# Attention and MLP on one core: half-width left sums in one bank, one key transpose a unit, and a re-ordered tail

## The chip, the cores and the metric

The kernel runs on one core of one Trainium2 chip. The metric is device time in microseconds of one execution. TensorE (PE in the profile, PEld for its weight loads) multiplies; VectorE (DVE), ScalarE (ACT) and GpSimd (POOL) do the element-wise work; SyncE (SP) and POOL issue most DMA transfers. The program gives each engine its own list of instructions, in an order written out by hand, with semaphores between the engines.

## The reference

```
q, k, v: (8, 12, 448, 64) fp32        batch, heads, sequence, head width
q_n = q / sqrt(mean(q*q) + 1e-6) * g_q        (over the head width)
k_n = k / sqrt(mean(k*k) + 1e-6) * g_k
attn = softmax(q_n @ k_n^T / 8)               448 x 448 for each head
x = concat over heads of (attn @ v)           (8, 448, 768)
xn = (x - mean) / sqrt(var + 1e-6) * g_ln     (LayerNorm over 768)
out = x + relu(xn @ w1) @ w2                  w1 768 x 3072, w2 3072 x 768
```

## The kernel before

**Pairs and steps.** Two heads make a pair; six pairs make a batch; 48 pairs in all, in units of one or two pairs that are loaded and prepared together. The 448 keys of a head are three blocks of 128 and a left block of 64; the two left blocks of a pair are stacked into one of 128. So a pair has seven steps: three blocks of head 0, three of head 1, and the common left block. Scores come out transposed, keys on the partitions and 448 queries along the row (`score`, L461); ScalarE takes the exponential into a row buffer E (`power`, L503); then E is the stationary operand of the value sums.

**Value sums** (`value`, L524 to L544). For each step there are four matmuls, with 128 columns of E as weights and 65 columns of values streamed (64 and a column of ones, for the softmax denominator); the seventh step streams 130, both heads at once. The first three go to query blocks 0, 1 and 2 in bank `oA`. The fourth takes E columns 320:448, a full width of 128, into bank `oB`; of its result only the lower half (queries 384:448) is used. There is one `oA` and one `oB`. After the seventh step `evac_o` (L546) takes the reciprocals of the denominators (L555, L556) and multiplies (L557, L562), into the batch's token tiles `x` (three tiles of 128 tokens) and `xl` (64 left tokens; two batches share one such tile). The next pair's first sum waits for that. The first batch's six pairs go by another function (L791), with banks of its own.

**Preparation of a unit** (`pieces`). Squares on ScalarE into `khl` (a, c), their sums on DVE (d, e), roots (g), keys weighted on POOL (i, L324), split into a high and a low half on POOL and DVE (j, k), queries scaled (l) and doubled (m). Then SP issues DMA transposes of keys (x, `dma_k`, L351 and L354) and queries (y, `dma_q`, L361 and L364), from the ninth unit on. Keys take three transfers: twelve groups at once, and the left groups in two halves of 64 partitions. The next unit's squares overwrite `khl`, so they wait for those transposes. `PLAN` gives each piece a step, counted from two pairs before the unit's first pair, the same for all units; Q, K and V in it are the loads (Q and K of the next unit, V of this one).

**MLP.** While attention of batch b + 1 runs, the MLP of batch b does (`run_rest`): it emits one product chunk (six matmuls), then as many attention steps as its share says, so that they are done `tails` chunks before the end of the batch's chunks. In the last chunks there is only the second product and, in pieces of `LN_AT`, LayerNorm of the next batch (`ln_list`). A batch with odd b has four token tiles (its own three and the shared left one), one with even b three. The up-product is L1126 with Relu on ScalarE (L1128). The down-product (`products`) goes by a seven-product scheme in place of eight for each two token tiles: sums of hidden halves are formed first (`sums_of`), and seven products are added into the two tiles with signs and shared terms, at chunk offsets given by `AFTER`. Product 1 is kept by a ScalarE copy (`keep`, L1238), products 6 and 7 are added to it (`second`, L1247), and `spread` (L1254) adds the kept sum into the tiles, one half of a tile at a time. For the second pair of tiles the kept sum lies in two row buffers of E.

**Where the order comes from.** It is all written by hand: `ORDER` for the first 110 us, then `PLAN`, `AFTER`, `LN_AT`, `tails` and the shares in `run_rest`.

Of the kernel before, what the change touches and what calls it, by code (L numbers as in the profile page):

```python
# [71 lines left out]
PLAN = [(-8, "bai"), (-7, "d"), (-6, "c"), (-5, "ej"), (-4, "g"), (-3, "lk"), (0, "QmKx"), (1, "V"), (2, "y")]  # L72
AFTER = ((2, 1, 5, 5, 7, 9, 9, 10, 10, 13, 11, 12, 14), (1, 2, 3, 5, 7, 7, 9, 10, 10, 11, 12, 15, 14), (1, 2, 5, 9, 8, 8, 9, 10, 10, 15, 14, 12, 14), (10, 14), (6, 7))
LN_AT = ((0, 3, 3, 6, 7), (0, 1, 2, 4, 4, 4))
# [49 lines left out]
class _Fast:  # L124
# [158 lines left out]
    def pieces(self, u):  # L283
# [64 lines left out]
        def dma_k():  # L348

            khl, kU = c["khl"].rearrange("p g e d -> p g (e d)"), self.kU[u % 2]  # L350
            nc.sync.dma_start_transpose(  # L351
                kU[:, 0:1536].rearrange("p (g c) -> p g c", c=128), khl[:, 0:12])
            for e in range(2):
                nc.sync.dma_start_transpose(  # L354
                    kU[:, 1536:1920].rearrange("p (w c) -> p w c", w=2)[
                        :, :, 128 * e:128 * e + D], khl[64 * e:64 * e + 64, 12:14])

        def dma_q():
# [6 lines left out]
            for w in range(2):  # L365
                self.prs[p0 + w] = dict(
                    q=qU[:, w].rearrange("p e s -> p (e s)"),
                    main=self.kU[u % 2][:, 768 * w:768 * w + 768],
                    left=self.kU[u % 2][:, 1536 + 192 * w:1728 + 192 * w])
# [110 lines left out]
    def left_score(self, p):  # L480
# [8 lines left out]
        for e in range(2):  # L489
            nc.tensor.matmul(ps[64 * e:64 * e + 64, 0:S], left[:, 128 * e:128 * e + 64],  # L490
# [28 lines left out]
    def values(self, p, i):  # L519
        self.value(p, i)  # L520
        if i == 6:
            self.evac_o(p)

    def value(self, p, i):  # L524
# [6 lines left out]
        oA, oB = c["oA"], c["oB"]  # L531
        if i < 6:
            h, j = divmod(i, 3)
            rhs = self.v16[:, p % 6, h, j]
            cs = slice(65 * h, 65 * h + 65)
        else:
            rhs = self.vl[:, p % 6].rearrange("p e d -> p (e d)")
            cs = slice(0, 130)
        for t in range(3):
            nc.tensor.matmul(oA[:, t, cs], E[:, ts(t, 128)], rhs,  # L540
                             start=(i == 0 and t == 0), stop=(i == 6 and t == 2))
        nc.tensor.matmul(oB[:, cs], E[:, 320:448], rhs, start=(i == 0), stop=(i == 6))  # L542
# [3 lines left out]
    def evac_o(self, p):  # L546
# [5 lines left out]
        oA = c["oA"].rearrange("p t (e d) -> p t e d", e=2)  # L552
        oB = c["oB"].rearrange("p (e d) -> p e d", e=2)
        rec = self.rec[:, p]
        nc.vector.reciprocal(rec[:, 0:3], oA[:, :, :, D])  # L555
        nc.vector.reciprocal(rec[64:128, 3], oB[64:128, :, D])  # L556
        nc.vector.tensor_tensor(  # L557
            out=x[:, :, 128 * hp:128 * hp + 128].rearrange("p t (e d) -> p t e d", e=2),
            in0=oA[:, :, :, 0:D], in1=rec[:, 0:3].unsqueeze(3).broadcast_to([128, 3, 2, D]),
            op=ALU.mult)  # L560
        r0 = 64 * (b % 2)
        nc.vector.tensor_tensor(  # L562
            out=xl[r0:r0 + 64, 128 * hp:128 * hp + 128].rearrange("p (e d) -> p e d", e=2),
            in0=oB[64:128, :, 0:D], in1=rec[64:128, 3].unsqueeze(2).broadcast_to([64, 2, D]),
            op=ALU.mult)
# [407 lines left out]
    def attention(self):  # L973
# [3 lines left out]
        for u in range(4, nu):  # L977
# [3 lines left out]
            for at, names in PLAN:  # L981
# [12 lines left out]
        for p in range(nb0, n + 1):  # L994
            for i in range(7):
                c = []
                if i == 0 and p < n and p % NPAIR == 0 and p > nb0:
# [14 lines left out]
                if p > nb0 + 1 and i == 1 and (p - 1) % NPAIR and p > 2 * NPAIR:  # L1012
# [122 lines left out]
    def after_up(self, b, f):  # L1135
# [4 lines left out]
        if f in (8, 14):  # L1140
            self.sums_of(0, "3", slice(0, 6) if f == 8 else slice(6, 12), self.xn)
        if f == 20:
# [29 lines left out]
    def products(self, b, n):  # L1172
# [51 lines left out]
        homes, flat = {}, self.rows.rearrange("p k s -> p (k s)")  # L1224

        def kept(a):
# [4 lines left out]
            return six(flat[:, S * homes[a]:S * homes[a] + 768].bitcast(FP32))  # L1231

        def keep(key, a):
            def call():
                if a:
                    k = homes[a] = next(k for k in range(8) if {k, k + 1} <= set(self.free_rows))
                    self.free_rows = [y for y in self.free_rows if y not in (k, k + 1)]
                nc.scalar.activation(kept(a), six(c[key][:, 0:384]), AFT.Identity)  # L1238
            return call

        def leave(a):
            self.free_rows += [homes[a], homes[a] + 1]

        def second(key, a):
            def call():
                u = kept(a)
                tt(out=u, in0=six(c[key][:, 0:384]), in1=u, op=ALU.add)  # L1247
                self.free(c.pop(key))
            return call

        def spread(t, g, a):
            def call():
                u, x = kept(a), six(tiles[t][:, 384 * g:384 * g + 384])
                stt(out=x, in0=u, scalar=self.rs[:, b, t:t + 1], in1=x, op0=ALU.mult, op1=ALU.add)  # L1254
# [15 lines left out]
        def pair(a):  # L1270
# [10 lines left out]
            places = dict(zip(("S2", "r1", "r2", "S4", "r5", "s5", "u2", "x2", "u3", "y3", "z3", "r4", "r3"), at))  # L1281
            if a == 0:
                after(h, lambda: self.sums_of(0, "1", slice(6, 12)))
            after(h + 1, keep(key(1), a))
            todo_of = dict(
                S2=sums(a, "2"), r1=read(key(1), a, L), r2=read(key(2), a, L), S4=sums(a, "4"),
                r5=read(key(5), a, R, last=False), s5=read(key(5), a + 1, R), u2=second(key(6), a),
                x2=spread(a, 1, a), u3=second(key(7), a), y3=spread(a + 1, 0, a), z3=spread(a + 1, 1, a),
# [3 lines left out]
            if a:  # L1292
# [319 lines left out]
```

## Time and profile before

| | |
|---|---|
| three runs | 612.62, 608.44, 611.16 us (median 611.16) |
| profiled execution, its own time | 609.88 us |
| its span | 608.3 us |
| granted TensorE clock, mean | 0.99 |
| TensorE busy | 566.9 us, 93% |
| VectorE, ScalarE, GpSimd busy | 398.3, 345.1, 249.7 us |
| matmuls | 4827 |

In the profile's rows, a line such as L542 is the line of the kernel that issued the instruction, `out<-in` are the program's buffers, a form such as `128*64 128x448` is the width of the weights (rows of the array by columns) and the streamed result, and `x4` counts merged instructions. Times in a timeline row are its start and its length in us. Matmuls overlap: a row's length holds its whole passage through the array, so the pitch of a stream is read from one start to the next. In a list of waits the three figures are us in total, how often, and the longest.

### The profile page before, as it was taken

What the parts mean: (1) busy time and instruction counts of PE and PEld (TensorE: products, weight loads), DVE (VectorE), ACT (ScalarE), POOL (GpSimd) and SP (SyncE); (2) the same over time, 40 slices, a digit from 0 to 9 for tenths busy, and PEclk for the clock granted to TensorE, in tenths of its full rate; (3) what the DMA queues carried; (4) which work ended last, traced back from release to release, by engine and by line L of the source; (5) the groups of instructions that cost most, each with busy time, mean ns of one, the idle gap of its engine ahead of it and who ended that gap; (6) DMA issues with size and microseconds to landing.
All of it is one profiled execution on the core that took longest, in us unless ns stands there. A gap on an engine that the chain in (4) does not pass through costs nothing.

```text
span 608.3 us, 12421 instructions
## 1 busy us (share of the span) xinstructions
PE 566.9 (93%) x4827; PEld 348.8 (57%) x4827; DVE 398.3 (65%) x798; ACT 345.1 (57%) x661; POOL 249.7 (41%) x309
## 2 busy tenths in 40 slices
PE   5999999999999898899999969889999999989995
PEld 4898876545665554445565636544556566644463
DVE  6999688398898267944399445863559843670174
ACT  5998773488634585168742858417874288214400
POOL 3648460064573567344572626725447230010000
PEclk9999999999999999999999979989999999999999
DMA  8999993483994996926858699965489560040011
GB/s 251 214 241 222 220 236 70 105 188 59 105 164 119 131 115 107 154 89 82 137 99 129 116 73 137 106 154 106 74 102 120 148 86 5 1 129 2 1 52 55
DMA packets 153282, 71.58 MB, mean 118 GB/s; under 512 B 124804, under 2 KB 145412, under 8 KB 153220
## 3 DMA queue, kind: packets, MB, share of 16 engines
q0 software_dynamic: 45936, 35.31, 37.1%
q1 hardware_dynamic: 107120, 35.23, 32.5%
q8 instruction: 39, 0.64, 0.5%
q10 hardware_dynamic: 164, 0.21, 0.2%
q14 instruction: 23, 0.19, 0.1%
HBM read 52.30 MB, written 11.01 MB: 104 GB/s over the span
## 4 chain that ended last, share of the span: by engine, by line
PE 63%; DVE 19%; DMA 7%; ACT 3%; SPq 2%; POOL 2%; issue 2%; DVEq 0%; ACTq 0%; POOLq 0%
PE psH L1126 26%; PE psC L1185 16%; PE psS L461 5%; PE psC L1331 4%; DMA kU<-khl 4%; PE oA L540 4%; DVE xn L1077 3%; PE psU L817 2%; DVE ssq L316 2%; DVE stat L1057 2%; POOL khl L113 2%; DMA v<-in_v_dram 2%; DVE x L1203 2%; DVE x L557 1%; DMA xnT<-xn 1%
## 5 line engine op out<-in xcount | busy, mean ns | idle before, releaser
L1126 PE MATMUL psH<-xnT,w 128*128 128x512 f16 (+1 forms) x1008 | 219.6, 359 | 9.5 <-ACT hT L1128 7.9
L503 ACT ACTIVATE room<-psS,rr_all 128x448 f16<-128x448 f32 x264 | 161.8, 630 | 52.0 <-PE psS L461 51.5
L1128 ACT ACTIVATE hT<-psH 128x512 f16<-128x512 f32 (+1 forms) x168 | 92.8, 552 | 116.1 <-PE psH L1126 102.4
L1126 PEld LDWEIGHTS <-w 128*128 128x128 f16 x1008 | 91.5, 98 | 87.7 <-issue 14.5
L1185 PEld LDWEIGHTS <-hT 128*128 128x128 f16 x996 | 94.1, 98 | 71.3 <-issue 14.9
L1185 PE MATMUL psC<-w,hT 128*128 128x384 f16 (+1 forms) x684 | 122.4, 326 | 8.9 <-DVE x L1203 4.2
L461 PE MATMUL psS<-qU,kU 128*128 128x448 f16 x252 | 86.8, 354 | 1.1 <-ACT room L503 1.1
L540 PEld LDWEIGHTS <-room 128*128 128x128 f16 x792 | 53.4, 98 | 41.1 <-DVE x L557 5.5
L324 POOL TENSOR_TENSOR room<-room,gprod 128x896 f32<-128x896 f32 x19 | 40.8, 2146 | 80.3 <-ACT khl L119 79.5
L540 PE MATMUL oA<-v,room 128*128 128x65 f16 x756 | 58.4, 194 | 3.8 <-DVE x L557 3.8
L316 DVE TENSOR_REDUCE ssq<-khl 128x14 f32<-128x896 f32 x35 | 37.8, 1079 | 31.3 <-ACT khl L119 31.1
L1185 PE MATMUL psC<-room,hT 128*128 128x384 f16 x312 | 55.8, 326 | 2.6 <-DVE x L1203 1.7
L555 DVE RECIPROCAL rec_all<-oA 128x6 f32<-128x6 f32 x42 | 8.1, 193 | 71.0 <-PE oA L540 70.6
L262 POOL DMA_DIRECT2D v<-in_v_dram x64 | 48.5, 763 | 5.6 <-PE oB L542 3.8
L1203 DVE SCALAR_TENSOR_TENSOR x<-psC,rs_all,x 128x384 f32<-128x384 f32 (+1 forms) x65 | 38.5, 606 | 15.1 <-PE psC L1185 13.7
L119 ACT ACTIVATE khl<-room 128x896 f32<-128x896 f32 x33 | 31.3, 947 | 29.6 <-DMA kU<-khl 23.4
L1350 POOL DMA_DIRECT2D out_dram<-x x18 | 10.4, 580 | 89.8 <-DVE x L1254 47.4
L542 PE MATMUL oB<-v,room 128*128 128x65 f16 x252 | 45.2, 194 | 0.3
L113 POOL CAST khl<-room 128x896 f16<-128x896 f32 x17 | 24.5, 1442 | 38.9 <-DVE ssq L316 32.3
L461 PEld LDWEIGHTS <-kU 128*128 128x128 f16 x252 | 24.4, 98 | 15.2 <-issue 0.3
L1166 DVE TENSOR_TENSOR hT<-hT 128x768 f16<-128x768 f16 (+1 forms) x18 | 11.5, 641 | 29.1 <-ACT hT L1128 29.0
L94 DVE SCALAR_TENSOR_TENSOR qn<-room,rr_all 128x256 f16<-128x256 f32 (+1 forms) x66 | 23.7, 418 | 10.1 <-ACT rr_all L320 10.1
(219 smaller groups left out, 821.1 us busy)
## 6 DMA issues: line engine op xcount, KB each, us to landing
out_dram<-x POOLq DMA_DIRECT2D x18, 384.0 KB, 2.8
room<-in_q_dram POOLq DMA_DIRECT2D x15, 384.0 KB, 4.4
room<-in_k_dram POOLq DMA_DIRECT2D x15, 384.0 KB, 5.6
w<-in_moe_w_ch_dram POOLq DMA_DIRECT2D x3, 1536.0 KB, 14.6
w<-in_moe_w_ch_dram POOLq DMA_DIRECT2D x8, 576.0 KB, 13.4
v<-in_v_dram POOLq DMA_DIRECT2D x64, 48.0 KB, 6.0
room<-in_q_dram SPq DMA_DIRECT2D x6, 384.0 KB, 9.5
room<-in_v_dram SPq DMA_DIRECT2D x5, 384.0 KB, 10.6
```

What stands on the lines that cost most here:

```text
L113: eng.tensor_copy(out=out, in_=x)
L262: self.nc.gpsimd.dma_start(out[:, h, :, 0:D], self.v[b, hs + h, 0:384].rearrange("(p j) d -> p j d", j=3))
L316: nc.vector.tensor_reduce(out=c["ssq"][:, n], in_=c["sq", n], axis=AX.X, op=ALU.add)
L324: _on(nc, f"i{u}", "P").tensor_tensor(out=self.loads[u][1], in0=self.loads[u][1], in1=sh.gprod.unsqueeze(1).broadcast_to([128, g, D]), op= ...
L461: self.nc.tensor.matmul(ps[:, 0:S], c["main"][:, ts(i, 128)], c["q"][:, ts(i // 3, S)], start=True, stop=True)
L503: self.nc.scalar.activation(out=o, in_=c.pop(("ps", i))[:, 0:S], func=AFT.Exp, scale=self.units[u][3][:, g:g + 1], bias=EXP_BIAS)
L540: nc.tensor.matmul(oA[:, t, cs], E[:, ts(t, 128)], rhs, start=(i == 0 and t == 0), stop=(i == 6 and t == 2))
L542: nc.tensor.matmul(oB[:, cs], E[:, 320:448], rhs, start=(i == 0), stop=(i == 6))
L1126: nc.tensor.matmul(ps[:, 0:N], sh.w1[:, dc, ts(f, 128)], xnT[:, dc, 0:N], start=(dc == 0), stop=(dc == NDC - 1))
L1128: nc.scalar.activation(out=hT[:, f, 0:N], in_=ps[:, 0:N], func=AFT.Relu)
L1185: nc.tensor.matmul(c[key][:, cols], x(f), y(f)[:, cols], start=(start and f == 0), stop=(stop and f == nf - 1))
L1203: stt(out=x, in0=c[key][:, c0:c0 + cols.stop - cols.start], scalar=self.rs[:, b, t:t + 1], in1=x, op0=ALU.mult, op1=ALU.add)
```

## The change

- **Keys**: one DMA transpose a unit for all 14 groups; the left keys of the two heads of a pair then lie 64 columns apart (`step=D`), where they were 128 apart.
- **Value sums**: a pair's sums all lie in one bank of 455 columns, `oA` for even pairs and `oB` for odd ones. The fourth matmul has 64 columns of E (384:448) as weights and writes 64 partitions: the lower ones for head 0, the upper ones for head 1; in the seventh step there are two such. It stands second, between query block 0 and query block 1.
- **Evacuation**: one reciprocal of seven columns; the left tokens are multiplied head by head.
- **Down-product**: product 1 goes to both halves of its tile at once, product 6 is added straight from its bank, and the sum of products 1, 6 and 7 goes to both halves of the second tile (one instruction for four tiles). The kept sum of the second pair of tiles lies in token tile 1, after that has been stored. New offsets.
- **Order**: `PLAN` has six variants, by the unit's number; key and query loads of the next unit are apart from each other, the value load comes at step 8 or 9 where it came at 1. After odd batches up to five steps of the next batch's attention are spread over the tail (`EXTRA`); shares, `tails`, `LN_AT` and `UP_AT` are new. The token tile is opened at the seventh step of a batch's second pair.
- `EVAC_AT` is 0, so the evacuation stays right behind the seventh step, and the statistics stay where they were.

```diff
-PLAN = [(-8, "bai"), (-7, "d"), (-6, "c"), (-5, "ej"), (-4, "g"), (-3, "lk"), (0, "QmKx"), (1, "V"), (2, "y")]
-LN_AT = ((0, 3, 3, 6, 7), (0, 1, 2, 4, 4, 4))
+EVAC_AT, STATS_AT = 0, 1
+UP_AT = (8, 12, 19)
+EXTRA = (0, 5)
+KEEP_AT, PUT_AT = (2, 1)
+PLAN = ([(-8, "bai"), (-7, "d"), (-6, "c"), (-5, "e"), (-4, "gjk"), (-3, "l"), (-1, "mK"), (1, "Qx"), (2, "y"), (9, "V")],
+        [(-8, "bai"), (-7, "d"), (-6, "c"), (-5, "ej"), (-2, "gk"), (-1, "lm"), (0, "K"), (1, "Qx"), (2, "y"), (8, "V")],
...
+LN_AT = ((0, 5, 5, 7, 9), (0, 2, 3, 4, 4, 5))
...
             nc.sync.dma_start_transpose(
-                kU[:, 0:1536].rearrange("p (g c) -> p g c", c=128), khl[:, 0:12])
-            for e in range(2):
-                nc.sync.dma_start_transpose(
-                    kU[:, 1536:1920].rearrange("p (w c) -> p w c", w=2)[
-                        :, :, 128 * e:128 * e + D], khl[64 * e:64 * e + 64, 12:14])
+                kU[:, 0:1792].rearrange("p (g c) -> p g c", c=128), khl)
...
-            c["oA"] = self.ps_o.tile([128, 3, 130], FP32, tag="oA", name="oA")
-            c["oB"] = self.ps_o.tile([128, 130], FP32, tag="oB", name="oB")
+            c["o"] = self.ps_o.tile([128, 455], FP32, tag="oB" if p % 2 else "oA", name="o")
...
-        for t in range(3):
-            nc.tensor.matmul(oA[:, t, cs], E[:, ts(t, 128)], rhs,
-                             start=(i == 0 and t == 0), stop=(i == 6 and t == 2))
-        nc.tensor.matmul(oB[:, cs], E[:, 320:448], rhs, start=(i == 0), stop=(i == 6))
+        for t in (0, None, 1, 2):
+            if t is not None:
+                nc.tensor.matmul(o[:, 130 * t + cs:130 * t + cs + 65 * len(heads)], E[:, ts(t, 128)], rhs,
+                                 start=(i == 0 and t == 0), stop=(i == 6 and t == 2))
+                continue
+            for e in heads:
+                nc.tensor.matmul(o[64 * e:64 * e + 64, 390:455], E[:, 384:S], rhs[:, 65 * e:65 * e + 65] if i == 6 else rhs,
+                                 start=False, stop=False)
...
-        nc.vector.reciprocal(rec[:, 0:3], oA[:, :, :, D])
-        nc.vector.reciprocal(rec[64:128, 3], oB[64:128, :, D])
+        nc.vector.reciprocal(rec[:, 0:7], o[:, :, D])
...
-        nc.vector.tensor_tensor(
-            out=xl[r0:r0 + 64, 128 * hp:128 * hp + 128].rearrange("p (e d) -> p e d", e=2),
-            in0=oB[64:128, :, 0:D], in1=rec[64:128, 3].unsqueeze(2).broadcast_to([64, 2, D]),
-            op=ALU.mult)
+        for e in range(2):
+            r = slice(64 * e, 64 * e + 64)
+            nc.vector.tensor_tensor(
+                out=xl[r0:r0 + 64, 128 * hp + 64 * e:128 * hp + 64 * e + 64], in0=o[r, 6, 0:D],
+                in1=rec[r, 6:7].broadcast_to([64, D]), op=ALU.mult)
...
-            return six(flat[:, S * homes[a]:S * homes[a] + 768].bitcast(FP32))
+            return six(tiles[1][:, 0:384])
...
-        def spread(t, g, a):
+        def spread(t, a):
             def call():
-                u, x = kept(a), six(tiles[t][:, 384 * g:384 * g + 384])
-                stt(out=x, in0=u, scalar=self.rs[:, b, t:t + 1], in1=x, op0=ALU.mult, op1=ALU.add)
+                u = kept(a)
+                if n == 4:
+                    twice(t, u.rearrange("p k s -> p (k s)"))
+                    return
+                for g in range(2):
+                    x = six(tiles[t][:, 384 * g:384 * g + 384])
+                    stt(out=x, in0=u, scalar=self.rs[:, b, t:t + 1], in1=x, op0=ALU.mult, op1=ALU.add)
...
-        tails = (13, 12)
+        tails = (13, 14)
...
-            share = [c if i < NFF else (1.15, 0.95)[b % 2] * c for i, (c, _) in enumerate(chunks)]
+            share = [c if i < NFF else (1.1, 0.85)[b % 2] * c for i, (c, _) in enumerate(chunks)]
...
+                if done > total:
+                    upto(int(goal + EXTRA[b % 2] * (done - total) / (sum(share) - total)))
```

More of the change, by code (lines that the diff above doesn't have):

```diff
@@ L489, in left_score @@
         for e in range(2):
-            nc.tensor.matmul(ps[64 * e:64 * e + 64, 0:S], left[:, 128 * e:128 * e + 64],
+            at = c.get("step", 2 * D) * e
+            nc.tensor.matmul(ps[64 * e:64 * e + 64, 0:S], left[:, at:at + D],
                              q[:, ts(e, S)], start=True, stop=True)
@@ L980, in attention @@
             s = 7 * (UNIT_PAIR[u] - 2)
[L981 removed]
+            for at, names in PLAN[u % 6]:
                 for y in names:
@@ L1230, in kept, with second @@
                 return six(rows)
-            return six(flat[:, S * homes[a]:S * homes[a] + 768].bitcast(FP32))
+            return six(tiles[1][:, 0:384])
         def keep(key, a):
[L1234 to L1244, printed above, removed]
+            return lambda: nc.scalar.activation(kept(a), six(c[key][:, 0:384]), AFT.Identity)
+        def second(key, a, last):
             def call():
```

53 lines of the change are left out of this document (28 added, 25 removed), and 4 rows, old and new, of the table PLAN.

## The prediction

> **What bounds the kernel now.** I read the page's busy table first, then the granted clock, then the list of waits, and last the order of TensorE's instructions inside one attention step.
>
> ```profile
> span 608.3 us, 12421 instructions
> PE 566.9 (93%) x4827; PEld 348.8 (57%) x4827; DVE 398.3 (65%) x798; ACT 345.1 (57%) x661; POOL 249.7 (41%) x309
> PEclk9999999999999999999999979989999999999999
> ```
>
> TensorE is busy for 93% of the span and no other engine passes 65%. Outside its waits, whatever lengthens TensorE's own stream lengthens the run. A busy share is not enough, though: TensorE's ends are modelled, so I go by the distance from one start to the next. Between two streamed matmuls of an attention step (score, three sums, fourth sum, next product) it is:
>
> ```profile
> 153.02 0.35 PE L461 MATMUL psS<-qU,kU 128*128 128x448 f16 x1
> 153.21 0.25 PE L540 MATMUL oA<-v,room 128*128 128x65 f16 x3
> 153.31 0.19 PE L542 MATMUL oB<-v,room 128*128 128x65 f16 x1
> 153.33 1.46 PE L1126 MATMUL psH<-xnT,w 128*128 128x512 f16 x6
> ...
> 157.20 0.33 PE L540 MATMUL oA<-vl,room 128*128 128x130 f16 x3
> 157.37 0.22 PE L542 MATMUL oB<-vl,room 128*128 128x130 f16 x1
> 157.43 0.35 PE L461 MATMUL psS<-qU,kU 128*128 128x448 f16 x1
> ```
>
> A 448-column score holds TensorE for 0.19 us (153.02 to 153.21). The four value sums of a step, 65 columns each, take 0.12 us together (153.21 to 153.33), 0.03 each. The seventh step, with 130 columns, takes 0.23 us (157.20 to 157.43), near 0.06 each. The waits that TensorE has left are few:
>
> ```profile
> ACT khl L119 <- DMA kU<-khl: 23.4, 7, 7.2
> PE psH L1126 <- ACT hT L1128: 7.9, 2, 5.0
> PE psC L1185 <- DVE x L1203: 5.9, 6, 2.5
> PE oA L540 <- DVE x L557: 3.8, 2, 2.0
> ```
>
> The columns are us in total, times, longest. The second row is ScalarE's Relus standing behind the key transposes of the first; the third lies at the LayerNorm boundaries; the fourth is the wait for the single pair of value banks. TensorE's three are 17.6 us, near the most that better order can win.
>
> **The fourth value sum.** This is the term that decides. Before, all four sums of a step load 128 columns of weights (the fourth takes E columns 320:448 and throws half of the result away). Afterwards the fourth loads 64 columns and writes 64 partitions, between the first full sum and the second. The trace has this kind of neighbourhood only where the left keys are scored (L490, form 128*64). Into it, and out of it:
>
> ```profile
> 89.72 0.26 PE L540 MATMUL oA<-v,room 128*128 128x65 f16 x3
> 89.81 0.19 PE L542 MATMUL oB<-v,room 128*128 128x65 f16 x1
> 89.93 0.57 PE L490 MATMUL psS<-qU,kU 128*64 128x448 f16 x4
> ...
> 195.41 0.35 PE L490 MATMUL psS<-qU,kU 128*64 128x448 f16 x2
> 195.70 0.27 PE L540 MATMUL oA<-v,room 128*128 128x65 f16 x3
> 195.81 0.19 PE L542 MATMUL oB<-v,room 128*128 128x65 f16 x1
> ```
>
> Entry: a 65-column full-width sum is followed after 0.12 us (89.81 to 89.93) where 0.03 is usual, so +0.09. Exit: the last two half-width scores run side by side, and the next full-width sum starts 0.29 us after them (195.41 to 195.70) where 0.19 is usual, so +0.10. Of the three sums behind the exit the first is slower too (195.70 to 195.81 is 0.11 for three, 0.02 more than at 89.72). Weight loads show the same hole:
>
> ```profile
> 195.01 0.37 PEld L490 LDWEIGHTS <-kU 128*64 128x64 f16 x6 [0.32 <-issue]
> 195.70 0.14 PEld L540 LDWEIGHTS <-room 128*128 128x128 f16 x3 [0.32 <-issue]
> ```
>
> The load idles 0.32 us before either side, with no semaphore named: the next weights aren't brought in ahead across the change of width. So I take 0.19 us more for each of the first six steps (0.31 in place of 0.12). For the seventh: entry and exit, the two halves of the fourth sum side by side at 0.03 instead of one of 0.06, so +0.16. The count:
>
> ```profile
> L542 PE MATMUL oB<-v,room 128*128 128x65 f16 x252 | 45.2, 194 | 0.3
> ```
>
> 252 is 42 pairs by six steps (the first batch's six pairs go by another function that isn't changed). Per pair 6 x 0.19 + 0.16 = 1.30 us; by 42, **+55 us**, in TensorE's own stream, with nothing beside it. Below, rounding gives 0.18 a step, 53 us; above, an exit 0.03 longer, which the slower first sum suggests, 63 us. I take 55, since the entry row is for the very same 65 columns.
>
> The Trainium skill, TensorEngine Tiling (Array Packing), Key Properties, says that a change of tiling mode (unlike a change of tile within a mode) drains TensorE, which speaks against this edit, and gives no time for it; the rows above agree, with 0.09 and 0.10 us. If a drain were the whole warm latency of a lone matmul, (398 + N) / 2.4 ns by the Trainium skill, TensorE: Matmul & The Clock Gate, Single matmul latency, an estimate would be 0.17 us a switch and near 98 us in all; the rows have 0.10 at most, and the measurement decides.
>
> **Two banks in turn.** Each pair's sums go to one bank, alternately, so a pair's first sum no longer waits for the last pair's division: the 3.8 us of L540 behind L557 go. What is late next there is the prep chain, which the longer steps cover. −3.8.
>
> **Key transposes.** Three SP transfers a unit become one, for the 17 units from the ninth on (51 transfers).
>
> ```profile
> kU<-khl SPq DMA_TRANSPOSE x51, 5.8
> ...
> 366.05 1.55 SPq L351 DMA_TRANSPOSE kU<-khl  x1
> 367.70 2.46 SPq L354 DMA_TRANSPOSE kU<-khl  x2
> ...
> 212.23 1.14 PE L1126 MATMUL psH<-xnT,w 128*128 128x384 f16 x6 [2.92 <-ACT hT L1128]
> 359.33 0.48 PE L1126 MATMUL psH<-xnT,w 128*128 128x384 f16 x1 [5.03 <-ACT hT L1128]
> ```
>
> Twelve groups take SP 1.55 us; fourteen would take 1.8, so about 2.2 of 4.0 us go, between 0 (if the transfer is bound by bytes) and 2.5. Queries wait behind keys on SP, and the next unit's squares wait on ScalarE for khl, with the Relus queued behind them. That chain releases 2.2 us sooner, and some five attention steps between transfer and squares are each 0.19 us longer. The 2.9 us stall goes, the 5.0 us one falls to about 2: −6. The granted clock after the longer stall was
>
> ```profile
> 350.00:360.00 10.00, 4.97 (x42) 3.05 (x40) 2.29 (x6) 2.74 (x6) 1.75 (x3) 0.86 1.85 111
> 360.00:370.00 10.00, 10.00 (x70) 5.58 (x69) 7.85 (x19) 8.90 (x19) 6.92 (x10) 0.80 0.38 88
> ```
>
> 0.86 and 0.80 (third figure from the end). At 0.80 ten busy us lose 2, and half of the window before another 0.5: −2.5 with the shorter stall. **The order of the unit transfers.**
>
> ```profile
> v<-in_v_dram POOLq DMA_DIRECT2D x64, 48.0 KB, 6.0
> ```
>
> Values load seven or eight steps later, still thirteen steps ahead of use, near 20 us at some 1.6 us a step (0.31 and a product of 1.3), against 6.0 us to land; keys and queries shift by a step or two. On POOL the value issues move behind the next unit's weighting of keys (L324), which is not late. 0, between −2 and +3 if a key load lands after its squares are due.
>
> **Evacuation.** One reciprocal for two (L555, L556), and two 64-by-64 products for one 64-by-128 (L562):
>
> ```profile
> L556 DVE RECIPROCAL rec_all<-oB 64x2 f32<-64x2 f32 x42 | 7.3, 173 | 1.3
> L562 DVE TENSOR_TENSOR xl<-oB,rec_all 64x128 f32<-64x128 f32 x42 | 12.3, 294 | 1.3
> ```
>
> −0.17 us and between +0.06 and +0.29 a pair: nothing, under TensorE, with DVE 65% busy. **The seventh product** goes to both halves in one instruction where there are four tiles; so does product 1, and product 6 is read from its bank.
>
> ```profile
> L1254 DVE SCALAR_TENSOR_TENSOR x<-xnT,rs_all,x 128x384 f32<-128x384 f32 x12 | 7.0, 611 | 0.1
> L1217 DVE SCALAR_TENSOR_TENSOR x<-psC,rs_all,x 128x768 f32<-128x768 f32 x3 | 3.0, 1006 | 0.0
> ```
>
> Four adds of 0.61 us become two of 1.01 and one of 0.61, +0.2 us of DVE for each two tiles; behind TensorE's longer steps that is 0, at most 0.4 at a boundary. But the kept sum of the second pair of tiles now lives in token tile 1, so ScalarE's copy must wait until that tile's store has landed:
>
> ```profile
> out_dram<-x POOLq DMA_DIRECT2D x18, 384.0 KB, 2.8
> ```
>
> 2.8 us from issue to landing, and the store is issued two chunks, over 2 us, before the copy. Queued behind the copy are the exponentials of the extra steps, and TensorE's scores behind those: 0 to 3 us at each of three boundaries, below nothing being excluded since a wait is only added. I take +2 in all. **Attention beside LayerNorm**: after odd batches up to five steps fill the tail.
>
> ```profile
> 184.59 2.11 PE L1185 MATMUL psC<-room,hT 128*128 128x384 f16 x12 [0.89 <-DVE xl L1203]
> ...
> 476.12 4.09 PE L1185 MATMUL psC<-room,hT 128*128 128x384 f16 x24 [0.80 <-DVE x L1203]
> ...
> 215.40 0.35 PE L461 MATMUL psS<-qU,kU 128*128 128x448 f16 x1 [0.44 <-ACT room L503]
> ```
>
> The tails' waits, near 0.9 us at each of three, may go, and short score waits like that at 215.40 are covered by longer steps: between 0 and −4, taken −3. After even batches nothing changes.
>
> **Sum.** 55 − 3.8 − 6 − 2.5 + 2 − 3 = 41.7. On the profiled execution's 609.9 us (span 608.3; the median of the three runs, 611.16, is 1.3 above it) that gives 651.6: **652 us**.
>
> **Rivals.** (1) *The half-width sum costs no switch*, because what the rows at 89.93 and 195.70 show belongs to the left scores alone (other weights, 448 columns). Then −13 us remain: **597 us**, at worst 606 if the prep and store terms fail. For it: only left scores, and a few early transposes, show the form. Against it: the entry is measured behind a 65-column sum, and both widths lose alike. Its deciding point: 13 us over 42 x 7 x 2 = 588 switches, 0.022 us each; below that the change wins, and the rows have four times that. Chance 0.10. (2) *The clock goes too.* If the pauses, two per step of some 1.5 us, count as idleness, TensorE may get 0.80 of its clock as it did from 360 to 370 us, over the 440 us from the first quoted step at 89 us to about 530: +110, **about 760 us**. Against it:
>
> ```profile
> 210.00:220.00 10.00, 6.89 (x53) 3.94 (x53) 7.49 (x16) 9.12 (x20) 5.04 (x6) 1.00 0.59 50
> ```
>
> 31% idle, in pieces of up to 2.9 us, left the clock at 1.00. The Trainium skill, TensorE: Matmul & The Clock Gate, Part 1, gates the clock after an idle window of about 3.4 us; the 5.0 us and 2.9 us stalls fall on either side of that. Chance 0.03. (3) *The stalls stay*: prep and store order give nothing back, and the exit costs 0.03 more: 609.9 + 63 − 4 = **669 us**; it is the upper end of the forecast, with its chance inside it.
>
> **Chances and range.** Forecast 0.87, rivals 0.10 and 0.03. The forecast's own range: low, 53 less 18 (all stalls gone) is 645, and I go to 638 for stalls that longer steps may cover at the boundaries; high, 669 and a little for new waits, 672. That holds about 0.92 of 0.87, so 0.80; the range is 638 to 672. One per cent, 6 us, is about what a measurement of this kernel can tell from no change. Rival 1 is faster by more than that in 0.07 and within it in 0.03; all else is slower: 0.90.
>
> **What would show it.** In the changed profile: the new sum in form 128*64, 0.12 us before it and after it; a step's value sums at 0.31 us instead of 0.12; weight loads "issue"-idle beside them; TensorE's stream longer in every attention stretch, not in the last 55 us; no wait of a first sum for the division; the stalls at 212 and 359 us gone or short; 17 key transfers. If the four sums still take 0.12 us, the forecast is wrong at its first step. If they take 0.31 and the time is under 638, the stalls covered more than I allowed.

## The result, and the profile after

The changed kernel takes 646.6 us (median of four runs, 644.75 to 649.74) where the kernel before takes 611.8 us: a ratio of 1.0585, with a 95% interval of 1.0522 to 1.0648. It is slower, as forecast, 5 us under the 652 us predicted and inside the range. The profiled execution of the changed kernel took 644.75 us, that of before 609.88; the accounts below compare these two. Each later run has runs of the kernel before beside it (medians of 607.39 to 609.45 us), and its ratio refers to those. Medians are over all executions of a kernel, while ratios and their intervals leave out those that ran slower at a lower granted clock.

The head of the page of the changed kernel, and the shares of its chain that ended last:

```profile
span 643.2 us, 12397 instructions
PE 623.3 (97%) x4869; PEld 368.6 (57%) x4869; DVE 406.3 (63%) x790; ACT 351.1 (55%) x661; POOL 243.9 (38%) x309
PEclk9999999999999999999999999999999999999999
PE 88%; DVE 7%; SPq 2%; DMA 1%; issue 1%; ACT 0%; DVEq 0%
```

TensorE is busy for 97% of the span in place of 93%, has 88% of the chain, and has a granted clock of 0.9 or more in every slice (0.998 in the mean; before 0.990). For the kernel before the chain's shares were these:

```profile
PE 63%; DVE 19%; DMA 7%; ACT 3%; SPq 2%; POOL 2%; issue 2%; DVEq 0%; ACTq 0%; POOLq 0%
```

So the run got longer while TensorE waited less: the other engines' part of the chain shrank from 37% to 12%, and TensorE's own stream grew. The timeline of TensorE in the changed kernel shows where. It starts at the first full-width sum of one of the first six steps, and then of a seventh step:

```profile
162.13 0.19 PE L546 MATMUL o<-v,room 128*128 128x65 f16 x1
162.25 0.22 PE L550 MATMUL o<-v,room 128*64 128x65 f16 x1
162.41 0.23 PE L546 MATMUL o<-v,room 128*128 128x65 f16 x2
162.48 1.46 PE L1140 MATMUL psH<-xnT,w 128*128 128x512 f16 x6
...
166.14 0.22 PE L546 MATMUL o<-vl,room 128*128 128x130 f16 x1
166.29 0.22 PE L550 MATMUL o<-vl,room 128*64 128x65 f16 x2
166.44 0.29 PE L546 MATMUL o<-vl,room 128*128 128x130 f16 x2
166.56 0.35 PE L466 MATMUL psS<-qU,kU 128*128 128x448 f16 x1
```

From start to start: 0.12 us into the half-width sum (162.13 to 162.25), 0.16 us out of it (162.25 to 162.41), and 0.07 us for the two full-width sums that are left. Over all 252 such places the medians are 0.123 us in and 0.151 us out, so the 0.16 of these rows is rounded up. The step takes 0.35 us (162.13 to 162.48) where it took 0.12; the seventh takes 0.42 (166.14 to 166.56) where it took 0.23. The list of waits of the changed kernel names no engine for it:

```profile
PEld L550 <- issue: 46.1, 217, 0.3
...
ACT x L1246 <- DMA out_dram<-x: 18.4, 3, 13.6
...
PE psC L1199 <- DVE x L1231: 4.3, 3, 1.5
PE psC L1199 <- DVE x L1217: 3.2, 5, 0.9
```

The weight loads of the half-width sum (L550) stand idle for 46.1 us in 217 places with nothing to wait for that the profile shows. TensorE's own waits in this stretch of the run are 7.5 us, all at the LayerNorm boundaries (L1199); those for the Relus (7.9 us before), for the division (3.8) and for the scores (1.1) are gone.

Added up over both traces, with each value sum counted from its start to the start of the matmul behind it, and TensorE's idle time in between put into a row of its own (the 3.8 us ahead of the first matmul, alike in both, are left out):

| | before | after | difference |
|---|---|---|---|
| value sums, streaming | 43.1 us | 106.5 us | +63.4 |
| value sums, TensorE waiting in that time | 9.0 us | 0.0 us | −9.0 |
| all else, from the first matmul's start to the last's | 546.1 us | 527.6 us | −18.5 |
| after that | 6.4 us | 5.4 us | −1.0 |

That is +34.9 us, the whole of the difference between the two profiled executions. TensorE's idle time in all went from 35.2 to 14.7 us, so of the 18.5 us some 11.5 are waits too (20.5 less the 9.0 of the second row), and 7 us are faster streaming. The loss lies in the attention stretch: from the first value sum in question to the last it is 479.8 us before and 517.5 us after, and behind the last one 79.3 and 76.7.

### The profile page after: what moved, and what is told of

The parts are those of the page before. It is cut to its first block, busy times and chain, and to the rows that moved or that the text cites. A ratio compares the mean times of both kernels' runs of the same rounds, so it can differ in the third digit from the quotient of the medians.

```text
span 643.2 us, 12397 instructions
## 1 busy us (share of the span) xinstructions
PE 623.3 (97%) x4869; PEld 368.6 (57%) x4869; DVE 406.3 (63%) x790; ACT 351.1 (55%) x661; POOL 243.9 (38%) x309
## 3 DMA queue, kind: packets, MB, share of 16 engines
q1 hardware_dynamic: 106032, 35.23, 28.5%
## 4 chain that ended last, share of the span: by engine, by line
PE 88%; DVE 7%; SPq 2%; DMA 1%; issue 1%; ACT 0%; DVEq 0%
PE psH L1140 30%; PE psC L1199 22%; PE o L546 10%; PE psS L466 7%; PE o L550 7%; PE psU L826 4%; PE psC L1339 4%; DVE xn L1091 2%; PE psS L496 1%; DVE stat L1071 1%; PE psS L768 1%; SPq L215 1%; SPq L223 1%; PE oA L800 1%; DMA xnT<-xn 1%
## 5 line engine op out<-in xcount | busy, mean ns | idle before, releaser
L509 ACT ACTIVATE room<-psS,rr_all 128x448 f16<-128x448 f32 x264 | 163.8, 630 | 91.0 <-PE psS L466 82.6
L1199 PEld LDWEIGHTS <-hT 128*128 128x128 f16 x996 | 93.1, 98 | 64.2 <-issue 9.3
L1199 PE MATMUL psC<-w,hT 128*128 128x384 f16 (+1 forms) x684 | 120.1, 323 | 7.5 <-DVE x L1231 4.3
L546 PE MATMUL o<-v,room 128*128 128x65 f16 x756 | 99.8, 198 | 0.0
L563 DVE RECIPROCAL rec_all<-o 128x7 f32<-128x7 f32 x42 | 8.6, 204 | 102.7 <-PE o L546 102.7
L546 PEld LDWEIGHTS <-room 128*128 128x128 f16 x792 | 51.9, 98 | 27.5 <-issue 2.1
L1199 PE MATMUL psC<-room,hT 128*128 128x384 f16 x312 | 55.6, 326 | 0.0
L550 PE MATMUL o<-v,room 128*64 128x65 f16 x252 | 54.9, 218 | 0.0
L550 PEld LDWEIGHTS <-room 128*64 128x64 f16 x276 | 28.1, 106 | 45.3 <-issue 41.4
L1358 POOL DMA_DIRECT2D out_dram<-x x18 | 10.4, 580 | 76.7 <-DVE x L1264 66.8
L103 DVE SCALAR_TENSOR_TENSOR qn<-room,rr_all 128x256 f16<-128x256 f32 (+1 forms) x66 | 26.4, 459 | 11.2 <-ACT rr_all L329 11.1
L1091 DVE SCALAR_TENSOR_TENSOR xn<-x,stat,gln 128x768 f16<-128x768 f32 x22 | 26.7, 1216 | 3.8 <-DMA xnT<-xn 3.6
```

What stands on the lines that cost most here:

```text
L509: self.nc.scalar.activation(out=o, in_=c.pop(("ps", i))[:, 0:S], func=AFT.Exp, scale=self.units[u][3][:, g:g + 1], bias=EXP_BIAS)
L546: nc.tensor.matmul(o[:, 130 * t + cs:130 * t + cs + 65 * len(heads)], E[:, ts(t, 128)], rhs, start=(i == 0 and t == 0), stop=(i == 6 and t ...
L550: nc.tensor.matmul(o[64 * e:64 * e + 64, 390:455], E[:, 384:S], rhs[:, 65 * e:65 * e + 65] if i == 6 else rhs, start=False, stop=False)
L1091: nc.vector.scalar_tensor_tensor(out=c["xn", t], in0=tiles[t], scalar=mv[:, t, 0:1], in1=sh.gln, op0=ALU.subtract, op1=ALU.mult)
L1199: nc.tensor.matmul(c[key][:, cols], x(f), y(f)[:, cols], start=(start and f == 0), stop=(stop and f == nf - 1))
```

## The experiments

The theory was that of the prediction: each change between 128 and 64 columns of weights costs TensorE a tenth of a us, twice a step, and the rest of the change is worth some 13 us the other way. Its rivals: the half-width sums are dear in themselves (64 partitions, an instruction more), or the new order and the new bank are to blame.

### The half-width sum at full width

```diff
-                nc.tensor.matmul(o[64 * e:64 * e + 64, 390:455], E[:, 384:S], rhs[:, 65 * e:65 * e + 65] if i == 6 else rhs,
+                nc.tensor.matmul(o[:, 390:455], E[:, 320:S], rhs[:, 65 * e:65 * e + 65] if i == 6 else rhs,
```

> The changed kernel with one thing altered: the fourth sum takes 128 columns of E (320:448) as weights and writes all 128 partitions of the same 65 columns; number, order and streamed columns of the matmuls stay. (The left tokens' sums of both heads are mixed by this, so their result is left out of the computation; the work is the same.) Theory S (change of width): the 588 switches, which in the changed trace make the value sums 106.5 us long against 43 us without waits before, go, -63 us; stalls that the longer steps covered come back by 3 to 12 us: 585 to 594 us, value sums near 43 us. Rival O (the new order of loads, tail and stores is what costs): the sums get shorter but the waits take the time back, 635 to 647 us.

Measured: 593.85 us, 0.9808 of before (0.9713 to 0.9904). The same instructions in the same order, in this kernel's timeline of TensorE:

```profile
150.53 0.19 PE L546 MATMUL o<-v,room 128*128 128x65 f16 x1
150.56 0.20 PE L550 MATMUL o<-v,room 128*128 128x65 f16 x1
150.59 0.22 PE L546 MATMUL o<-v,room 128*128 128x65 f16 x2
150.65 1.46 PE L1140 MATMUL psH<-xnT,w 128*128 128x512 f16 x6
```

The step is at 0.12 us again (150.53 to 150.65); all value sums stream for 42.7 us in place of 106.5. So neither the order nor the bank nor the number of instructions costs anything: the width does, 63.8 us for 588 changes, 0.108 us each. The run gives back only 51 of these us (profiled 593.8 against 644.75), because TensorE waits 8.8 us more (23.5 us idle in place of 14.7), and its mean clock is 0.991 in place of 0.998, which is 4 us of 592. In this kernel's list of waits some rows are back that the changed kernel had lost:

```profile
PE psC L1199 <- DVE x L1231: 6.7, 3, 3.6
PE psS L466 <- ACT room L509: 5.4, 3, 2.9
```

### Few changes of width in place of many

The half-width sums are left as they are, but gathered: those of steps 0 and 1 run in step 1, those of 2 and 3 in step 3, the last three in step 6. A pair has 6 changes of width in place of 14, 252 in all in place of 588.

```diff
-            for e in heads:
-                nc.tensor.matmul(o[64 * e:64 * e + 64, 390:455], E[:, 384:S], rhs[:, 65 * e:65 * e + 65] if i == 6 else rhs,
+            for y in {1: (0, 1), 3: (2, 3), 6: (4, 5, 6)}.get(i, ()):
+                Ey = c["EL"] if y == 6 else c["E"][y]
+                for e in (heads if y == 6 else (y // 3,)):
+                    nc.tensor.matmul(o[64 * e:64 * e + 64, 390:455], Ey[:, 384:S],
+                                     rhs[:, 65 * e:65 * e + 65] if y == 6 else self.v16[:, p % 6, e, y % 3],
```

> The changed kernel with the half-width sums gathered: those of steps 0 and 1 at step 1, of 2 and 3 at step 3, of 4, 5 and 6 at step 6, so 6 changes of width a pair in place of 14, with the same number of half-width matmuls. S: 336 switches fewer at 0.108 us each (63.4 us over 588) is -36 us, and 2 to 8 us of stalls come back: 608 to 617 us, value sums near 70 us. Rival H (the price belongs to each half-width sum, by its form or by its half of the bank, not to the change of width): as many such sums, so 640 to 648 us, value sums near 106 us.

Measured: 610.6 us, 1.0049 (1.0009 to 1.0089). Its TensorE timeline, first a step without a half-width sum, then a seventh step with all four of its group:

```profile
156.73 0.25 PE L546 MATMUL o<-v,room 128*128 128x65 f16 x3
156.82 1.46 PE L1144 MATMUL psH<-xnT,w 128*128 128x512 f16 x6
...
158.40 0.22 PE L546 MATMUL o<-vl,room 128*128 128x130 f16 x1
158.55 0.22 PE L552 MATMUL o<-v,room 128*64 128x65 f16 x1
158.56 0.22 PE L552 MATMUL o<-vl,room 128*64 128x65 f16 x1
158.60 0.20 PE L552 MATMUL o<-v,room 128*64 128x65 f16 x1
158.64 0.19 PE L552 MATMUL o<-vl,room 128*64 128x65 f16 x1
158.76 0.29 PE L546 MATMUL o<-vl,room 128*128 128x130 f16 x2
```

Among themselves the half-width sums follow here at 0.01 to 0.04 us; only the way in (158.40 to 158.55, where 0.06 is usual behind a sum of 130 columns) and the way out (158.64 to 158.76) are dear. The value sums take 67.5 us, 39 less than in the changed kernel for 336 changes less: 0.116 us each, with as many half-width sums as before. The price belongs to the change of width and not to the half-width sum. What in the change takes the time (TensorE running empty, or weights that are not loaded ahead) these runs don't tell apart.

### The sums alone, and all but the sums

The value sums and the evacuation of the change, put alone into the kernel before; and the changed kernel with the value sums and evacuation of before (two single banks, full width).

```diff
-            c["oA"] = self.ps_o.tile([128, 3, 130], FP32, tag="oA", name="oA")
-            c["oB"] = self.ps_o.tile([128, 130], FP32, tag="oB", name="oB")
+            c["o"] = self.ps_o.tile([128, 455], FP32, tag="oB" if p % 2 else "oA", name="o")
...
-        nc.tensor.matmul(oB[:, cs], E[:, 320:448], rhs, start=(i == 0), stop=(i == 6))
+            for e in heads:
+                nc.tensor.matmul(o[64 * e:64 * e + 64, 390:455], E[:, 384:S], rhs[:, 65 * e:65 * e + 65] if i == 6 else rhs,
```

> The kernel before with the new value sums and evacuation alone. S: +63 us of switches less 9 us of waits at the first sums and up to 12 us of other stalls that longer steps cover: 652 to 664 us, above the changed kernel, since the rest of the change is a gain. O: 600 to 611 us.

> The changed kernel with the value sums and the evacuation of before (two banks, one of each, full width); key transpose, order, down-product and tail stay as changed. S: no switch, so 588 to 602 us, a few us above the kernel with one full-width bank because a pair's first sum waits for the division again (3.8 us before): faster than before by 1.5 to 4%. O: 635 to 650 us.

Measured: the sums alone 651.6 us, 1.0727 (1.0662 to 1.0793), just under the 652 to 664 expected, with 106.4 us of value sums and 18.4 us of idle time: the whole loss comes with them. Most of what is given back comes with them too. The value sums stream for 63 us more, the profiled execution (651.76 us) is 42 us longer, so some 21 us come back with no edit but the sums, their two banks and the evacuation, 16.8 of them in TensorE's idle time (35.2 before). This kernel keeps the three key transposes a unit, and still TensorE has no wait for a Relu, and ScalarE's squares wait once for the transposes where they waited seven times (23.4 us). In its list of waits:

```profile
ACT khl L119 <- DMA kU<-khl: 2.7, 1, 2.7
```

All but the sums: 606.76 us, 0.9933 (0.9878 to 0.9987), above the 588 to 602 expected. Most of the stalls were still there, 31.5 us of idle time, and the largest, 6.6 us, came from a key load that landed after its squares were due. In this kernel's timeline of ScalarE:

```profile
440.27 0.95 ACT L128 ACTIVATE khl<-room 128x896 f32<-128x896 f32 x1 [7.93 <-DMA room<-in_k_dram]
```

That is the new order of loads without the long steps that give a load its time: the term that the prediction had at 0 with a bound of +3.

### Two banks in turn alone, one key transpose alone

The kernel before with one bank a pair, in turn, all sums at full width, with the order of sums and the evacuation of the change; and the kernel before with one transpose for all 14 groups of keys.

```diff
             nc.sync.dma_start_transpose(
-                kU[:, 0:1536].rearrange("p (g c) -> p g c", c=128), khl[:, 0:12])
-            for e in range(2):
-                nc.sync.dma_start_transpose(
...
+                kU[:, 0:1792].rearrange("p (g c) -> p g c", c=128), khl)
```

> The kernel before with a pair's sums in one bank, two banks in turn, as in the change, but with the fourth sum at full width (128 columns; the left tokens' sums of both heads are mixed by this, so their result is left out of the computation; the work is the same). It measures the two banks alone. The prediction priced them at the 3.8 us of first sums waiting for the division; the two full-width variants of the changed kernel differ by 13 us in the same thing (593.9 against 606.8). If the waits named are all: 603 to 607 us against 609.4; if the single banks also hold back what is queued behind them, 594 to 602 us.

> The kernel before with one key transpose a unit in place of three, nothing else. The prediction's term: SP issues for 2.2 us less a unit, the 2.9 us stall goes and the 5.0 us stall falls by about half, and the clock loss behind it: -4 to -8 us, 601 to 606 us. If the transfers are bound by bytes or the order hides them: 607 to 611 us.

Measured: two banks 602.64 us, 0.9899 (0.9816 to 0.9982), which is −6.8 us where the prediction had −3.8. One transpose 606.46 us, 0.9972 (0.9934 to 1.0009): nothing that can be told from no change, where it had −6. The DMA row of the key transposes of this last kernel (issues, and median us from issue to landing; before it was 51 issues and 5.8 us):

```profile
kU<-khl SPq DMA_TRANSPOSE x17, 8.0
```

SP is free earlier (one issue of 2.23 us in place of 2.27 and 2.52), but the data come hardly sooner: the 5.8 us are those of each transfer by itself, and from a unit's first issue to its last landing it was 8.7 us (median of the 13 units for which the trace has the last landing), now 8.0 (11 units). In this kernel's timeline the stall near 359 us has shrunk from 5.0 to 1.2 us, and another has come 20 us later, which was not there:

```profile
353.28 1.14 PE L1123 MATMUL psH<-xnT,w 128*128 128x384 f16 x6 [1.18 <-ACT hT L1125]
...
373.78 0.35 PE L457 MATMUL psS<-qU,kU 128*128 128x448 f16 x1 [2.24 <-ACT room L500]
```

This kernel's ScalarE had waited 3.9 us for a key load just before. The 2.9 us stall near 212 us, which was to go, is still there at 2.6 us, and here too ScalarE's square now waits for a key load where it had waited for the transposes:

```profile
210.22 0.95 ACT L119 ACTIVATE khl<-room 128x896 f32<-128x896 f32 x1 [4.76 <-DMA room<-in_k_dram]
...
211.60 1.14 PE L1123 MATMUL psH<-xnT,w 128*128 128x384 f16 x6 [2.58 <-ACT hT L1125]
```

So the edit shortened one of its two stalls as the prediction said; the key loads, next in line behind the transposes, were not priced.

### The kept sum without the wait for the store

The kept sum of the second pair of tiles goes to a part of `hT` in place of token tile 1, so ScalarE's copy need not wait until the tile is stored.

```diff
-            return six(tiles[1][:, 0:384])
+            return self.hT[:, 0:6, 128:256].bitcast(FP32)
```

> The changed kernel with the kept sum of the second pair of tiles in a part of hT that is no longer read, where the change has token tile 1; so ScalarE's copy does not wait for that tile's store (18.4 us of such waits on ScalarE, and three waits of TensorE, 4.3 us, behind the add that follows). The kept sum is spread by two instructions there, 0.2 us more of DVE. If the store wait is what those three waits come from: -3 to -5 us, 640 to 644 us against 646.6. If DVE's queue is what is late there anyway: no change, 645 to 648 us.

Measured: 645.87 us, 1.0598 (1.0514 to 1.0682), the changed kernel's own time. The row of TensorE's wait at the boundary hardly moves (changed kernel: 4.3 us, 3 times). In this kernel's list of waits:

```profile
PE psC L1199 <- DVE x L1231: 4.4, 3, 1.6
```

So TensorE waits there for DVE's queue and not for the store. In the changed kernel DVE comes to it late, with two long additions one behind the other, out of a stretch from 343.5 us on in which it has no gap:

```profile
348.02 0.95 DVE L1182 TENSOR_TENSOR hT<-hT 128x1536 f16<-128x1536 f16 x1
349.00 1.02 DVE L1231 SCALAR_TENSOR_TENSOR x<-psC,rs_all,x 128x768 f32<-128x768 f32 x1
```

### Looking for the best of both

The change without its half-width sums, with the kept edit of the last experiment (run twice, each time beside its own runs of before), and, beside the second of these runs, the same without the kept edit:

> The changed kernel with the value sums and evacuation of before (full width, two single banks) and the kept sum in hT. Against the same without the second edit (606.8 us, three waits of 2.8, 3.8 and 1.4 us behind that add): 599 to 603 us if the store wait holds TensorE there; 605 to 608 us if not.

> The full-width variant of the changed kernel with the kept sum in hT (601.0 us before, ratio 0.988), now on one chip beside the same without that edit, and in more rounds. If the store wait costs the full-width kernel: 599 to 603 us, 3 to 7 us below its partner. If the difference seen before was the chips': 602 to 606 us, within 2 us of it.

> Its partner: the changed kernel with the value sums and evacuation of before, kept sum in token tile 1 as changed (606.8 us before, ratio 0.993). With the store wait: 604 to 609 us. Without: 602 to 606 us.

Measured: 600.96 us, 0.9876 (0.9796 to 0.9956), and again 601.98 us, 0.9875 (0.9819 to 0.9931); without the kept edit 604.1 us, 0.9857 (0.9782 to 0.9933), and in its first run above 0.9933 (0.9878 to 0.9987). These intervals overlap, so what the kept edit is worth at full width stays open in the times. In the traces TensorE's wait behind the add (PE psC behind DVE x L1228) is 8.0 and 9.5 us without the edit and 5.2 us in both runs with it, so with short steps the store does hold TensorE; of these 3 to 4 us some 2 come back as a wait for ScalarE's copy (2.2 and 1.7 us). Both versions beat the kernel before by about 1% and the changed kernel by 6 to 7%.

Two further attempts on it failed. First, a full-width sum in one bank whose weights hold the 64 columns beside 64 zeros; DVE copies the columns between zeros one step ahead. (Pairs 6 to 17 keep the sums of before.)

```diff
+                w = self.pads[:, at:at + 128] if e else self.pads[:, at + 64:at + 192]
+                nc.tensor.matmul(o[:, 390:455], w, rhs[:, 65 * e:65 * e + 65] if i == 6 else rhs,
...
+        if i < 6 or p + 1 < B * NPAIR:
+            self.pad(p + (i == 6), (i + 1) % 7)
```

> The changed kernel with no half-width sum left, and nothing of the computation left out: DVE copies each step's left 64 columns of E between two blocks of 64 zeros, one step ahead, and the fourth sum takes 128 columns of that, left and zeros for head 0, zeros and left for head 1, so a pair's sums still fit one bank, two in turn (for pairs 18 to 47; pairs 6 to 17 use the full-width sums and the two single banks of before). If the change of width is the cost, the value sums come to 43 to 46 us and the time near that of the mixed full-width variant, 594 us, with 0 to 8 us more for sums that wait for the copies: 594 to 602 us. If the one bank, the zero columns or the new order cost: above 606 us.

Measured: 622.47 us, 1.0271 (1.0239 to 1.0304). No change of width is left in the sums of pairs 18 to 47, but TensorE and DVE now wait for each other, in this kernel's list of waits:

```profile
DVE kU L574 <- PE o L562: 41.0, 46, 1.5
...
PE o L562 <- DVE kU L574: 25.1, 31, 1.8
```

L574 is the copy, L562 the sum. DVE's list has a fixed order: a copy that stands behind TensorE's sum of the step before holds up all DVE work behind it, and a copy that stands behind long DVE work holds up TensorE. DVE's busy time rose by 37 us over the first experiment's 398.2, to 435.1.

Second, the late key load moved one step after the halves of the keys (`k`) in each variant of `PLAN`:

```diff
-PLAN = ([(-8, "bai"), (-7, "d"), (-6, "c"), (-5, "e"), (-4, "gjk"), (-3, "l"), (-1, "mK"), (1, "Qx"), (2, "y"), (9, "V")],
+PLAN = ([(-8, "bai"), (-7, "d"), (-6, "c"), (-5, "e"), (-4, "gjk"), (-3, "lK"), (-1, "m"), (1, "Qx"), (2, "y"), (9, "V")],
...
```

> As the full-width variant with the kept sum in hT (601.0 us), and with the key load of the next unit one step after the keys of this one are used up, where the changed plan has it up to three steps later. That variant still has one stall of 4.6 us of TensorE at 438 us, behind a square on ScalarE that waits for keys. If the late key load is its cause, it goes: 594 to 599 us. If POOL, which issues the load, is late for another reason: 599 to 603 us.

Measured: 612.94 us, 1.0085 (1.0047 to 1.0122), above both expectations, and 2% above the same kernel without it (ratio 0.988). The stall at 438 us did go, as was expected if the late load was its cause: TensorE's scores wait 0.4 us for ScalarE in all, where it was 5.0. The timeline of POOL's queue and of DVE in this kernel, around the first of its new stalls:

```profile
196.05 0.82 POOL L215 DMA_DIRECT2D room<-in_k_dram  x1
...
198.03 0.63 POOL L1355 DMA_DIRECT2D out_dram<-x  x1
...
205.32 0.56 DVE L563 TENSOR_TENSOR x<-oA,rec_all 128x384 f32<-128x384 f32 x1 [7.78 <-issue]
...
205.94 0.35 PE L546 MATMUL oA<-v,room 128*128 128x65 f16 x3 [6.26 <-DVE x L563]
```

The key load now stands ahead of the store of the token tile, and the next division into that tile comes 7.8 us late, with TensorE behind it for 6.3 us (a second time, 6.8 us, at 353 us). The profile names only "issue" for it, but the trace has the landings: the store issued at 198.03 us landed at 205.24, and the second, issued at 344.96, at 352.72, each 0.08 us ahead of the division (205.32 and 352.80). They took 7.2 and 7.8 us where the median of this kernel's stores is 3.1. So it is the store that the division waits for.

## Why the prediction was right, and where its steps were off

**The fourth value sum** was the right term with the right mechanism, and 8 us too small: +63.4 us where it had +55, with 63 as its upper bound. The entry came out as read from the rows (0.12 us, +0.09). The exit was the mis-sized part: 0.15 us to the next sum where the prediction had 0.13, and the two full-width sums behind it 0.07 where it had 0.06, hence 0.35 a step and not 0.31. It knew of the slower first sum behind an exit and put it into the bound and not into the value; that the entry row is for the same 65 columns, the reason it gave for the lower value, says nothing about the exit. The seventh step was +0.19 where it had +0.16. (The term's lower bound, at 0.18 us a step, adds up to 52 us and not 53, which moves nothing else.) The Trainium skill, TensorEngine Tiling (Array Packing), Key Properties, says that a change of tiling mode drains TensorE. That it costs time is borne out, with a mean of 0.108 us a change here and 0.116 by the gathered kernel; that the time is a drain is not shown. The estimate of 0.17 us, by which a drain would be a lone matmul's whole latency, is not borne out.

**What the rest gives back** was the term most off: −13.3 us forecast, −28.5 measured. The step that failed is the sentence that TensorE's three quoted waits, 17.6 us, are near the most that better order can win. TensorE's idle time was 35.2 us, spread over many smaller rows, and it fell by 20.5, to 14.7. The reason is one that the prediction named and priced only for the prep chain: 42 pairs with 1.5 us more of TensorE's own work give every other engine time. The kernel with the sums alone shows it: some 21 of the 28.5 us come back there with no edit but the sums, their banks and the evacuation. The first experiment shows it from the other side: take the 64 us of changes out, and 8.8 us of waits come back. Both errors are of one kind, the sizes of two opposite terms, and they offset each other to 5 us of 652. That is luck in part: with the sums at the predicted 55 us, and the rest as measured, the forecast would have been 636 us, under the lower end of the range.

Part by part: **two banks** were worth −6.8 us alone (−3.8 forecast), though with an interval of 1 to 11 us. **Key transposes**: the 5.0 and 2.9 us stalls did go in the changed kernel, where TensorE has no wait for a Relu left; but they are gone with the sums alone too, which keep the three transposes (the two banks alone leave 9.1 us of these waits), and the one transpose alone gives nothing that can be measured. So the long steps are enough for the −6, and the transpose is not. **The clock** rose from 0.990 to 0.998, 0.008 of 608 us or some 5 us against the 2.5 forecast; that fits most of the 7 us of faster streaming in size, and in the first experiment the clock fell back together with the waits, but no run changes the clock alone. **The store** of the kept sum's tile cost nothing that can be measured where +2 was taken: ScalarE does wait for it, 18.4 us in three times, but the experiment that takes this wait away changes neither the time nor TensorE's wait. **Attention beside LayerNorm**: the short score waits went (with the sums alone they are gone too), the tails' waits did not (1.4 to 1.5 us at each of the three boundaries, DVE's long additions last), so the −3 came from elsewhere. **The order of the loads** cost nothing in the changed kernel; with short steps it has a 6.6 us stall. **Evacuation**, two products of 0.219 us in place of one of 0.294, was hidden, as forecast.

The rivals: (1) fell by the first two experiments, since the price is there, it is the width's, and it is five times the 0.022 us at which the change would have won. With its condition met, in the first experiment, the time is 593.85 us, near its 597. (2) fell by the clock, 0.998 with 588 pauses. (3) fell by the idle time; its price for the switches, 63 us, was right, its claim that the stalls stay was wrong.

## What to carry to other kernels

Before weights of half the width go into a stream of short matmuls, price the change of width from two neighbouring starts in the trace, both the way in and the way out: here half the weights in one sum of 0.03 us cost 0.23 us a step. If the width must change, gather the narrow ones; here that alone took back more than 30 us. And when the bound engine's stream grows, expect its waits to shrink all over (here from 35.2 to 14.7 us of idle time), and not only in the few rows at the top of the list. A helper one step ahead on an engine whose list has a fixed order, or a load moved ahead of a store in one queue, makes a wait of its own.

## What the runs showed that was not expected

A weight load of 64 columns is not shorter than one of 128; it took 106 ns against 98, in these groups of the changed kernel:

```profile
L546 PEld LDWEIGHTS <-room 128*128 128x128 f16 x792 | 51.9, 98 | 27.5 <-issue 2.1
...
L550 PEld LDWEIGHTS <-room 128*64 128x64 f16 x276 | 28.1, 106 | 45.3 <-issue 41.4
```

The way out of the narrow form is dearer than the way in, 0.122 to 0.125 us over the usual pitch at most exits against 0.095 at the entries, where the prediction read 0.10 behind left scores of 448 columns. Pauses of a tenth of a us, 588 of them, leave the granted clock at 0.998. One transpose of 14 groups frees the issuing queue 2.6 us sooner than three transposes (1.8 us in place of 4.5, medians over 17 units), but its data land only 0.7 us sooner: 8.0 us after the first issue in place of 8.7.
